# A down product of a mixture-of-experts arm, cut into three parts that stand in three places

## The chip, the cores and the metric

The kernel runs on one core of a Trainium2 chip. The metric is the device time of one execution in microseconds (us). Before the change the median of 3 runs is 892.29 us (890.97 to 893.22).

## The reference

Three layers follow each other. What matters here is the second: each of 1792 tokens goes to the one expert of eight that its gate picks, if its skip score is positive.

```python
x = attn_out.transpose(0, 2, 1, 3).reshape(1792, 768)   # sigmoid attention, 12 heads
do_compute = (x @ w_skip) > 0
xc = x[do_compute]
probs = softmax(xc @ w_gate)                            # 8 experts
e_idx, gate_w = argmax(probs), max(probs)
for e in range(8):
    mask = e_idx == e
    h = np.maximum(xc[mask] @ w1[e], 0.0)               # 768 -> 1024
    y[mask] = gate_w[mask, None] * (h @ w2[e])          # 1024 -> 768
x[do_compute] = xc + y
# then a dense layer over all rows: g = elu(x @ w_in), out = g @ w_out   (768 -> 2048 -> 768)
```

With the inputs that are timed, the chosen tokens per expert are 0, 65, 199, 144, 391, 35, 10 and 222.

## The kernel before, in words

Every matrix product is made of three fp32r products (high by high, high by low, low by high), so that `gemm` (L593 to L596) issues three matmuls: L594, L595, L596.

The expert stage works on blocks of up to 256 tokens of one expert: two halves of 128 rows. A first block is taken early; the others are ordered by how many rows they hold, and a branch per block picks one of three arms. `k = 3` (the "many" arm) has more than 64 rows in the second half, `k = 2` (the middle arm, "few") has 1 to 64, `k = 1` has none. By the counts above, the blocks after the first are two "many" arms, two middle arms and three arms with one half. **Only the two middle arms execute changed code**; they are blocks 3 and 4.

The weights of an expert come in eight chunks of 128 x 1536: chunks 0 to 3 are the up weights, 4 to 7 the down weights. A chunk is loaded by SyncE (L550), and split into a high part on ScalarE (L585) and a low part on VectorE (L587). A down chunk holds 4 slices of 128 hidden rows and 384 output columns. Chunk 4, the fifth, holds hidden slices 0 to 3 and output columns 0 to 383.

A middle arm runs in this order on TensorE:

1. `up_parts`: the up products, first the full half (3 matmuls per slice, into `acc0` and `acc1`), then the few rows. The few rows' high and low parts stand side by side in one operand, so two matmuls per slice do for them (L959, L960).
2. `back` of chunks 4 and 5 for the few rows.
3. `h_columns(1)`: the turns of h. The second 512 hidden columns of the full half are transposed (L142, 4 matmuls) and those of the few rows turned and folded (L930, 4 matmuls of two passes each), into PSUM tiles `pt0` and `pt1`. ScalarE takes the relu and rounds it (L937), VectorE makes the low part (L938), both into the tile `both`.
4. `back` of chunks 6 and 7 for the few rows. These need what L938 wrote. After each of the two, ScalarE copies the sum to SBUF (L1027, `yf`).
5. `back` of chunk 4 for the full half: four slices of three matmuls, into `acc2`. Its inputs are hidden slices 0 to 3, turned much earlier, and the split chunk 4.
6. `outcome`: the fold. Two fp32 matmuls (L1094, two passes each) add the two parts of the few rows, from `yf` into `acc0` and `acc1`, and VectorE multiplies by the gate and adds to the rows (L1095, twice).

The other chunks of the full half (5, 6, 7) are done in the next block, beside its first steps.

Behind the arm comes the control flow. The arm that is not taken is replaced by `rest()`, a tiny matmul (L1257), ScalarE copy (L1258) and VectorE copy (L1259), which keep the semaphore counts of all paths alike. On each engine the sequencer jumps over the code of the untaken arms: L1275 is the branch of the "few" arm, L1279 that of the "many" arm, L1266 asks whether the next block has rows. The next block begins with transposes of its gathered rows (L142, out of `xg`) into `pt0`, `pt1` and `acc1`.

The order of the instructions on TensorE, ScalarE and VectorE is the order in which they are written (`manual_schedule`).

Of the kernel before, what the change touches and what calls it, by code (L numbers as in the profile page):

```python
# [23 lines left out]
P = 128  # L24
# [10 lines left out]
KF1 = F1 // P  # L35
# [6 lines left out]
N2 = DM // 2  # L42
WCH = 1536
# [48 lines left out]
def build(nc, tc, a):  # L92
# [3 lines left out]
    with ExitStack() as top:  # L96
# [44 lines left out]
        def flip(dst, src):  # L141
            nc.tensor.transpose(dst, src, ident)  # L142
# [34 lines left out]
        with ExitStack() as st:  # L177
# [411 lines left out]
            def weights(i, c):  # L589
                j = (8 * i + c) % NSPL  # L590
                return whi_t[j], wlo_t[j]

            def gemm(o, a_hi, a_lo, b_hi, b_lo, first, last):  # L593
                nc.tensor.matmul(o, a_hi, b_hi, start=first, stop=False)  # L594
                nc.tensor.matmul(o, a_hi, b_lo, start=False, stop=False)  # L595
                nc.tensor.matmul(o, a_lo, b_hi, start=False, stop=last)  # L596
# [159 lines left out]
            py = [[acc_t[j][:, :N2] for j in js] for js in ((2, 3), (4, 1))]  # L756
# [165 lines left out]
            def h_columns(nh, sizes):  # L922
                for h, n in enumerate(sizes):
                    pt = pt_t[(nh + h) % 2].rearrange("p (c n) -> p c n", c=4)[:, :, :n]
                    for j in range(4):
                        w = slice(j * P, (j + 1) * P)
                        if n == P:
                            flip(pt[:, j, :], hs_t[nh][:, w])
                        else:
                            nc.tensor.matmul(  # L930
                                pt[:, j, :], hf_t[nh][:, w], fold[:, :n], start=True, stop=True
                            )
                    t = slice(h * P, h * P + n)
                    h_hi, h_lo = h2[:, nh, 0, :, t], h2[:, nh, 1, :, t]
                    if n < P:
                        h_lo = h2[:, nh, 0, :, h * P + n : (h + 1) * P]
                    nc.scalar.activation(h_hi, pt, AF.Relu)  # L937
                    nc.vector.scalar_tensor_tensor(  # L938
                        h_lo, pt, 0.0, h_hi, op0=ALU.max, op1=ALU.subtract
                    )  # L940
# [4 lines left out]
            def h_part(s, k):  # L945
                return h2[:, k // 4, s, k % 4]

            def product(o, h, n, a2, i, c, width, k0, total):

                t = slice(h * P, (h + 1) * P)  # L950
                for j in range(WCH // width):
                    w = slice(j * width, (j + 1) * width)
                    hi, lo = (u[:, w] for u in weights(i, c))
                    a_hi, a_lo = (a2(s, k0 + j)[:, t] for s in range(2))
                    first, last = k0 + j == 0, k0 + j == total - 1
                    if n == P:
                        gemm(o, a_hi, a_lo, hi, lo, first, last)
                    else:
                        nc.tensor.matmul(o, a_hi, hi, start=first, stop=False, skip_group_check=True)  # L959
                        nc.tensor.matmul(  # L960
                            o[:n], a_hi[:, :n], lo, start=False, stop=last, skip_group_check=True
                        )
# [55 lines left out]
                        else:  # L1018
                            nc.scalar.copy(hf_t[nh], acc_t[(3, 0)[nh]])

            def back(i, h, n, chunks):

                for c in chunks:
                    c4, nh = divmod(c - 4, 2)
                    product(py[nh][h], h, n, h_part, i, c, N2, 4 * c4, KF1)
                    if n < P and c4:
                        nc.scalar.copy(yf_t[nh], py[nh][h])  # L1027

# [25 lines left out]
            def expert(i, k, sizes, following=None):  # L1054
                whole = sizes == (P, P)

                def soon():
                    outcome(i - 1, 0, P)

                if whole:  # L1060
                    up_two(i, soon)
                    ahead(i, 4)
                else:
                    up_parts(i, sizes, soon)
                    if len(sizes) > 1:
                        skips(f"many{i}", 1 - (k >> 1))
                    elif i + 1 < NB:
                        skips(f"more{i + 1}", (following + 3) >> 2)
                ahead(i, 5)
                for h, n in list(enumerate(sizes))[1:]:  # L1070
                    if whole:
                        back(i, h, n, range(4, 8))
                        outcome(i, h, n)
                        back(i, 0, P, range(4, 5))
                    else:
                        back(i, h, n, range(4, 6))
                        h_columns(1, sizes)
                        back(i, h, n, range(6, 8))
                        back(i, 0, P, range(4, 5))
                        outcome(i, h, n)  # L1080
                if len(sizes) == 1:
                    back(i, 0, P, range(4, 5))
                    h_columns(1, sizes)

            def outcome(i, h, n):
                gated(xg_t[i % NXG][h], slot_gate[:, 2 * i + h : 2 * i + h + 1], h, n)
# [441 lines left out]
```

## Time and profile before

| | us |
|---|---|
| median of 3 runs | 892.29 |
| the profiled execution | 889.8 |
| span of the profiled execution | 888.0 |
| busy TensorE in the span | 867.5 |
| first middle arm, up products to the last transposes of the next block | about 271 to 301 |
| second middle arm | about 307 to 336 |

The profile is one execution. A timeline row gives the start, the length, the engine, the line of the kernel, the operation with its output and inputs, and how often; in square brackets stands how long the engine was idle before it, and which instruction's end released it. The length of a matmul is modelled and overlaps the next one: the distance between starts tells the pace. Rows with "q" behind an engine's name are instructions of that engine's sequencer (PEldq is TensorE's), which are not counted as busy.

### The profile page before, as it was taken

To read this page: it belongs to the slowest core of one execution; us is meant where nothing else is said; L and a number is where in the kernel's file an instruction comes from. 1 tells how busy PE (TensorE), PEld (TensorE's weight loads), DVE (VectorE), ACT (ScalarE), POOL (GpSimd) and SP (SyncE) were. 2 spreads that over 40 slices of the span, in tenths; PEclk is the share of its full clock that TensorE was granted. 3 is DMA by queue.
4 is the path that set the end of the run, shared out by engine and by line. 5 is a ranking of instruction groups with operands and counts; after the bars stand their busy time and mean duration, and the time that the engine had idled before them with its cause. 6 is when DMAs were issued, how large, how long until landed. Compare 5 with 4: busy or idle time off the path is not lost.

```text
span 888.0 us, 13671 instructions
## 1 busy us (share of the span) xinstructions
PE 867.5 (98%) x5206; PEld 705.1 (79%) x5206; DVE 555.1 (63%) x872; ACT 476.3 (54%) x680; POOL 82.8 (9%) x79
## 2 busy tenths in 40 slices
PE   9999999999999899999999999999999999999998
PEld 6544454899998787888888888888888888888997
DVE  4878777886656648885888875443434434334664
ACT  7876776545346447764545454443443434434664
POOL 1000001021120213351000000000000100000100
PEclk9999999999999999999999999999999999999999
DMA  9898976789772538927733330100010100000100
GB/s 331 268 317 308 314 275 198 285 334 405 273 258 90 190 155 342 410 92 245 237 88 108 107 108 19 54 1 18 19 35 19 54 1 1 1 1 18 54 1 37
DMA packets 37842, 134.71 MB, mean 152 GB/s; under 512 B 5082, under 2 KB 9306, under 8 KB 37746
## 3 DMA queue, kind: packets, MB, share of 16 engines
q1 hardware_dynamic: 33122, 114.26, 36.0%
q0 software_dynamic: 4480, 19.01, 6.0%
q8 instruction: 56, 0.92, 0.4%
q14 instruction: 40, 0.33, 0.1%
q10 hardware_dynamic: 144, 0.20, 0.1%
HBM read 112.47 MB, written 23.99 MB: 154 GB/s over the span
## 4 chain that ended last, share of the span: by engine, by line
PE 54%; DVE 0%; ACT 0%; issue 0%; ACTq 0%
PE acc L1393 16%; PE pt L1393 10%; PE acc L1361 9%; PE acc L1362 9%; PE acc L1360 9%; PE acc L142 1%; PE acc L1244 0%; PE acc L594 0%; PE acc L596 0%; PE acc L595 0%; DVE both L611 0%; ACT both L609 0%; ACT raw L1404 0%; ACTq L1524 0%; ACTq L609 0%
## 5 line engine op out<-in xcount | busy, mean ns | idle before, releaser
L587 DVE TENSOR_TENSOR wlo<-raw,whi 128x1536 fp32r<-128x1536 f32 x64 | 111.4, 1758 | 29.4 <-ACT whi L585 28.8
L1371 DVE SCALAR_TENSOR_TENSOR m<-m,acc 128x512 f32<-128x512 f32 (+1 forms) x64 | 39.7, 620 | 139.4 <-ACT m L1370 139.4
L1369 ACT ACTIVATE m<-acc 128x512 f32<-128x512 f32 (+1 forms) x64 | 34.9, 545 | 168.6 <-PE acc L1362 158.6
L250 ACT ACTIVATE at<-ps,bias 128x896 f32<-128x896 f32 x96 | 82.7, 918 | 37.6 <-PE ps L297 34.7
L585 ACT CAST whi<-raw 128x1536 fp32r<-128x1536 f32 x64 | 94.0, 1482 | 16.2 <-PE acc L596 5.4
L1393 PE MATMUL acc<-wol,gh 128*128 128x256 f32 x320 | 100.8, 315 | 0.0
L1393 PE MATMUL acc<-woh,gl 128*128 128x256 f32 x320 | 100.4, 314 | 0.0
L1393 PE MATMUL acc<-woh,gh 128*128 128x256 f32 x320 | 100.4, 314 | 0.0
L1361 PE MATMUL acc<-x,wih 128*128 128x512 f32 (+1 forms) x270 | 96.2, 356 | 0.0
L1360 PE MATMUL acc<-x,wih 128*128 128x512 f32 (+1 forms) x270 | 96.2, 356 | 0.0
L1362 PE MATMUL acc<-x,wil 128*128 128x512 f32 (+1 forms) x270 | 96.1, 356 | 0.0
L594 PE MATMUL acc<-whi,both 128*128 128x384 f32 (+1 forms) x236 | 83.9, 355 | 1.8 <-DVE both L611 1.8
L595 PE MATMUL acc<-wlo,both 128*128 128x384 f32 (+1 forms) x236 | 82.9, 351 | 0.6 <-DVE wlo L587 0.6
L596 PE MATMUL acc<-whi,both 128*128 128x384 f32 (+1 forms) x236 | 82.6, 350 | 0.0
L1349 DVE TENSOR_TENSOR wol<-wo,woh 128x768 fp32r<-128x768 f32 x64 | 61.2, 956 | 23.4 <-ACT woh L1348 23.0
L1393 PEld LDWEIGHTS acc<-woh,gh 128*128 128x128 f32 x320 | 60.3, 188 | 10.0
L1393 PEld LDWEIGHTS acc<-wol,gh 128*128 128x128 f32 x320 | 60.3, 188 | 9.4
L1348 ACT CAST woh<-wo 128x768 fp32r<-128x768 f32 x64 | 53.4, 834 | 25.9 <-PE acc L1393 25.9
L1375 DVE TENSOR_TENSOR gl<-m,gh 128x512 fp32r<-128x512 f32 (+1 forms) x64 | 40.0, 626 | 40.5 <-ACT gh L1374 40.5
L1393 PEld LDWEIGHTS acc<-woh,gl 128*128 128x128 f32 x320 | 60.1, 188 | 4.2
L1343 DVE TENSOR_TENSOR wil<-wi,wih 128x768 fp32r<-128x768 f32 x60 | 57.4, 956 | 7.6 <-ACT wih L1342 6.9
L1374 ACT CAST gh<-m 128x512 fp32r<-128x512 f32 (+1 forms) x64 | 36.3, 567 | 46.0 <-DVE m L1371 46.0
(272 smaller groups left out, 1910.4 us busy)
## 6 DMA issues: line engine op xcount, KB each, us to landing
raw<-in_w SPq DMA_DIRECT2D x66, 768.0 KB, 12.0
raw<-in_wi SPq DMA_DIRECT2D x9, 768.0 KB, 5.6
raw<-in_wo SPq DMA_DIRECT2D x9, 768.0 KB, 6.7
raw<-in_wi SPq DMA_DIRECT2D x14, 384.0 KB
raw<-in_wo SPq DMA_DIRECT2D x14, 384.0 KB, 3.1
qr<-in_q SPq DMA_DIRECT2D x11, 448.0 KB, 6.9
vt<-in_v SPq DMA_DIRECT2D x12, 384.0 KB, 5.9
x_d<-xr SPq DMA_DIRECT2D x12, 384.0 KB, 6.5
```

The lines of the kernel that those rows point to most:

```text
L250: nc.scalar.activation(out, ps, AF.Sigmoid, bias=bias, scale=QK_SCALE)
L585: nc.scalar.copy(w_hi, raw)
L587: nc.vector.tensor_sub(w_lo, raw, w_hi)
L594: nc.tensor.matmul(o, a_hi, b_hi, start=first, stop=False)
L595: nc.tensor.matmul(o, a_hi, b_lo, start=False, stop=False)
L596: nc.tensor.matmul(o, a_lo, b_hi, start=False, stop=last)
L1343: nc.vector.tensor_sub(pair[1], raw, pair[0])
L1349: nc.vector.tensor_sub(pair[1], wo_r[f], pair[0])
L1360: nc.tensor.matmul(o, a, b, start=(cc == 0), stop=False)
L1361: nc.tensor.matmul(o, a, c, start=False, stop=False)
L1362: nc.tensor.matmul(o, wil[:, cc], b, start=False, stop=(cc == KD - 1))
L1393: nc.tensor.matmul(o, a, b, start=(clears and f == 0 and k_ == 0), stop=(f == KF2 - 1 and k_ == 2), skip_group_check=True,)
```

## The change

`product` and `back` take a slice of the four steps of a chunk. In the middle arm the full half's chunk 4 (twelve matmuls into `acc2`) is cut in three: two steps behind the turns of h and in front of the few rows' chunks 6 and 7, one step behind these, and one step behind the fold.

```diff
-            def product(o, h, n, a2, i, c, width, k0, total):
+            def product(o, h, n, a2, i, c, width, k0, total, part=slice(None)):
...
-                for j in range(WCH // width):
+                for j in range(WCH // width)[part]:
...
-            def back(i, h, n, chunks):
+            def back(i, h, n, chunks, part=slice(None)):
...
-                    product(py[nh][h], h, n, h_part, i, c, N2, 4 * c4, KF1)
+                    product(py[nh][h], h, n, h_part, i, c, N2, 4 * c4, KF1, part)
...
                         back(i, h, n, range(4, 6))
                         h_columns(1, sizes)
+                        back(i, 0, P, range(4, 5), slice(0, 2))
                         back(i, h, n, range(6, 8))
-                        back(i, 0, P, range(4, 5))
+                        back(i, 0, P, range(4, 5), slice(2, 3))
                         outcome(i, h, n)
+                        back(i, 0, P, range(4, 5), slice(3, 4))
```

Only TensorE's order changes; it has as many instructions as before, and those of the other engines stand as they stood. The lines of the changed kernel below the arm carry numbers that are higher by 2.

The first place is on TensorE behind the turns of h, in a middle arm. `acc2` is the full half's sum, `acc3` one of the few rows', `whi0`/`wlo0` the split chunk 4 and `whi2`/`wlo2` chunk 6.

```order
 L142 MATMUL pt1_1883<-cst_79,hs1_2297 128x128 x4
 L930 MATMUL pt0_1882<-cst_79,hf1_2299 128x64 x4
+L594 MATMUL acc2_1886<-whi0_1812,both_117 128x384
+L595 MATMUL acc2_1886<-wlo0_1813,both_117 128x384
+L596 MATMUL acc2_1886<-whi0_1812,both_117 128x384
+L594 MATMUL acc2_1886<-whi0_1812,both_117 128x384
+L595 MATMUL acc2_1886<-wlo0_1813,both_117 128x384
+L596 MATMUL acc2_1886<-whi0_1812,both_117 128x384
 L959 MATMUL acc3_1887<-whi2_1893,both_117 128x384
 L960 MATMUL acc3_1887<-wlo2_1894,both_117 64x384
```

Six matmuls now stand between the turns and the first matmul that needs what L938 makes of them.

The second place is on TensorE at the arm's end, where `acc0` and `acc1` take the fold, and the branch leaves the arm.

```order
-L594 MATMUL acc2_1886<-whi0_1812,both_117 128x384
-L595 MATMUL acc2_1886<-wlo0_1813,both_117 128x384
-L596 MATMUL acc2_1886<-whi0_1812,both_117 128x384
-L1094 MATMUL acc0_1884<-hf0_2298,cst_79 128x384
-L1094 MATMUL acc1_1885<-hf1_2299,cst_79 128x384
-L1275 UNCONDITIONAL_BRANCH
...
+L1096 MATMUL acc0_1884<-hf0_2298,cst_79 128x384
+L1096 MATMUL acc1_1885<-hf1_2299,cst_79 128x384
+L594 MATMUL acc2_1886<-whi0_1812,both_117 128x384
+L595 MATMUL acc2_1886<-wlo0_1813,both_117 128x384
+L596 MATMUL acc2_1886<-whi0_1812,both_117 128x384
+L1277 UNCONDITIONAL_BRANCH
```

The fold stood behind all twelve matmuls of chunk 4; now nine of the twelve stand before it, six of those before the few rows' last chunks, and three stand between the fold and the branch.

## Rows read from the trace of the kernel before

**Rows 1.** The page's head and its first part: busy us (share), instructions.

```profile
span 888.0 us, 13671 instructions
PE 867.5 (98%) x5206; PEld 705.1 (79%) x5206; DVE 555.1 (63%) x872; ACT 476.3 (54%) x680; POOL 82.8 (9%) x79
```

**Rows 2.** The instructions of L960: count, ns min/median/max, first and last start.

```profile
L960 PE MATMUL acc<-wlo,both x56: 332/337/394, 273.3 to 329.9; 128*64 128x384 f32 x32, 128*64 128x512 f32 x24
```

**Rows 3.** The timeline of TensorE, first middle arm, turns of h to next block.

```profile
289.29 1.00 PE L930 MATMUL pt<-cst,hf 128*128 128x64 f32 x8
291.23 0.44 PE L959 MATMUL acc<-whi,both 128*128 128x384 f32 x1 [0.94 <-DVE both L938]
...
294.12 0.34 PE L594 MATMUL acc<-whi,both 128*128 128x384 f32 x1
...
296.20 1.45 PE L1094 MATMUL acc<-hf,cst 128*128 128x384 f32 x4
297.49 0.17 PE L1257 MATMUL acc<-iota_h 128*128 128x2 f16 x1
299.37 1.06 PE L142 MATMUL pt<-cst,xg 128*128 128x128 f32 x8 [1.72 <-DVE rest L1259]
```

**Rows 4.** The same of the second middle arm.

```profile
325.24 1.00 PE L930 MATMUL pt<-cst,hf 128*128 128x64 f32 x8
327.18 0.44 PE L959 MATMUL acc<-whi,both 128*128 128x384 f32 x1 [0.93 <-DVE both L938]
...
330.05 0.34 PE L594 MATMUL acc<-whi,both 128*128 128x384 f32 x1
...
332.14 1.45 PE L1094 MATMUL acc<-hf,cst 128*128 128x384 f32 x4
333.43 0.17 PE L1257 MATMUL acc<-iota_h 128*128 128x2 f16 x1
334.57 1.09 PE L142 MATMUL pt<-cst,xg 128*128 128x128 f32 x8 [0.98 <-DVE rest L1259]
```

**Rows 5.** The timelines of VectorE and ScalarE, first middle arm.

```profile
290.12 1.05 DVE L938 SCALAR_TENSOR_TENSOR both<-pt,both 128x512 fp32r<-128x512 f32 x2
...
298.22 0.14 DVE L1259 COPY rest<-cst 128x1 f32<-128x1 f32 x1
...
294.37 0.48 ACT L1027 COPY hf<-acc 128x384 f32<-128x384 f32 x1 [0.61 <-PE acc L960]
```

**Rows 6.** The same of the second middle arm.

```profile
326.07 1.05 DVE L938 SCALAR_TENSOR_TENSOR both<-pt,both 128x512 fp32r<-128x512 f32 x2
...
334.37 0.15 DVE L1259 COPY rest<-cst 128x1 f32<-128x1 f32 x1
...
330.31 0.48 ACT L1027 COPY hf<-acc 128x384 f32<-128x384 f32 x1 [0.91 <-PE acc L960]
```

**Rows 7.** The timeline of TensorE behind the earlier turns of h.

```profile
281.74 1.00 PE L930 MATMUL pt<-cst,hf 128*128 128x64 f32 x8
282.56 0.48 PE L594 MATMUL acc<-whi,both 128*128 128x512 f32 x1
```

**Rows 8.** Branches of TensorE's sequencer (L1275, L1279) at the first middle arm's end.

```profile
L1275 PEldq COMPARE_BRANCH  x1: 218/218/218, 294.9 to 294.9; - x1
L1279 PEldq COMPARE_BRANCH  x2: 444/1816/3189, 295.2 to 295.7; - x2
```

**Rows 9.** Branches of L1279 at the second middle arm's end.

```profile
L1279 PEldq COMPARE_BRANCH  x2: 200/275/350, 331.1 to 331.5; - x2
```

**Rows 10.** Branches of L1279 from 225 to 262 us, the "many" arms.

```profile
L1279 PEldq COMPARE_BRANCH  x3: 63/197/201, 225.9 to 260.4; - x3
```

**Rows 11.** DMA queues from 295.7 to 298.9 us: packets, MB, share.

```profile
q8 instruction: 1, 0.02, 2.2%
```

**Rows 12.** What TensorE waited for from 335 to 412 us: total, times, longest.

```profile
PE pt L142 <- DVE both L938: 4.7, 3, 1.7
PE acc L594 <- DVE both L611: 1.8, 1, 1.8
```

## The prediction

> **What bounds the kernel now.** I read the busy table first: TensorE is busy 867.5 of 888.0 us, so it is the bound almost everywhere, and only its 20.5 us of idle time can be won by a change of order [rows 1]. Next, who runs the changed code: an instruction that only middle arms have, L960, ran 56 times, 24 on 512 and 32 on 384 columns, and one arm issues 12 and 16 [rows 2]. So there are two middle arms, and every gain or loss of mine is counted twice at most. Then TensorE's timeline through both arms [rows 3, 4]. Each shows two idle gaps. The first, behind the turns of h, is 0.94 and 0.93 us and ends when VectorE's L938 ends (290.12 + 1.05 = 291.17, and L959 starts at 291.23; in the second arm 327.12 and 327.18) [rows 3 to 6]. The second, at the start of the next block, is 1.72 and 0.98 us, and the profile puts both down to the VectorE copy L1259 [rows 3, 4].
>
> That releaser has to be checked against the copy's own end. In the second arm L1259 ends at 334.52 and the transposes start at 334.57: it is the releaser [rows 4, 6]. In the first arm it ends at 298.36, but the transposes start at 299.37, 1.0 us later [rows 3, 5]. What ended last there stands among the sequencer's branches: two branches of L1279, at 295.2 and 295.7 us, of 444 and 3189 ns. A sequencer takes one at a time, so the second is the long one: 295.7 to 298.9 [rows 8]. The same branches took 350 and 200 ns behind the second arm and at most 201 ns in the "many" arms [rows 9, 10]. In the long one's time the instruction queue moved one packet of 0.02 MB [rows 11]: the sequencer most likely waited for code. **So the two arms end on different things: the first on TensorE's own branch, the second on the chain fold, gate, L1259.**
>
> **Part by part.**
>
> *Six matmuls behind the turns.* The turns leave TensorE's pace 0.82 us after the start of L930's eight passes (281.74 to 282.56 with a matmul right behind) [rows 7]. So the first moved matmul can start at 289.29 + 0.82 = 290.11. One of this shape takes 0.173 us: twelve from 294.12 to 296.20 [rows 3]. It reads hidden slices turned long before, waits for nothing new, and after the gap may cost 0.1 more (0.44 against 0.34 for the first behind a gap) [rows 3]. Six last 1.04 to 1.14 and end at 291.15 to 291.25, against 291.23 where L959 is released anyway. They fit the gap; L938 itself does not move, as ScalarE and VectorE do nothing new. Cost: 0 to 0.07 us, since L959's weights can be loaded only once it is released. In the gap these six come free.
>
> *The wait that stays.* L959 still waits for L938, and behind it on TensorE stand the few rows' 16 matmuls. They start as before and last as before, 291.23 to 294.12, or 0.1 less if the engine is no longer coming out of a gap [rows 3].
>
> *Up to the fold.* Before, twelve matmuls stood between them and the fold; now three. The fold starts 9 x 0.173 = 1.56 us earlier, or 1.66 with the 0.1; I take 1.6. It needs both `yf` copies. The second ends at 294.85, or 0.1 earlier [rows 5]; the fold's first half then runs from about 294.6 for half of 1.29 us, so the second half, at 295.2, finds its copy done. No new wait, with 0.3 us to spare.
>
> *Behind the fold.* Three matmuls, 0.52 us, and L1257. Its start moves from 297.49 by 1.6 - 0.52 = 1.08 us to an earlier time. VectorE's two gate products and L1259 follow the fold and move by the whole 1.6 us; the three matmuls write another tile than they read, `acc2`.
>
> *Second arm.* The next block's transposes start at the later of three: L1259's end plus 0.05, so 334.57 - 1.6 = 332.97; TensorE's last matmul, 333.43 + 0.17 - 1.08 = 332.52; the sequencer. Its second branch of L1279 began at 331.5 and took at most 0.35 [rows 9]; in the first arm 0.47 us passed from the long branch's end (298.9) to the transposes [rows 3, 8], which makes it ready at about 332.3. The first branch, L1275, began at 294.9 in the first arm, 0.05 after the second `yf` copy ended [rows 5, 8]: the sequencer had stood at the fold and had everything in front of it issued. Now three matmuls come between the fold and that branch; none of my rows shows an issue alone, so I bound it by 0 and by their execution, 0.52. Ready then at 332.2 to 332.8: below 332.97 in either case. **Gain 1.6 us.**
>
> *First arm.* Here the long branch is the end. It moves with the second `yf` copy (0 to 0.1 earlier) and the three issues (0 to 0.52 later): between 0.1 earlier and 0.5 later. If it takes its 3.19 us again, the transposes start at 299.3 to 299.9 instead of 299.37. I take 0.2 later, near the middle. L1257 done 1.08 and L1259 done 1.6 us earlier then buy nothing. **Loss 0.2 us.**
>
> [...]
>
> *Behind the arms.* From 335 to 412 us TensorE waited for two things alone, L938 and L611 at the blocks' ends, 6.5 us in all [rows 12]: chains that start from TensorE itself and move with it. No wait there ends on a transfer, so a block that begins 1.4 us earlier passes it on to the dense stage. SyncE's loads and GpSimd's scatter behind L1259 start earlier too, by 1.6 us; nothing waits less or more for them.
>
> *Sum.* 1.6 - 0.2 = 1.4 us off the profiled execution, 889.8 to 888.4. The median stands 2.49 us above that execution; with the same shift, 892.29 to **890.9**.
>
> **The rivals.**
>
> A. *The long branch is gone in the new order.* For it: of seven branches of L1279 in [rows 8 to 10] one is long, and its timing against the fetches changes a little. Against it: the code is as long and the sequencer comes to it within half a microsecond of before. The first arm would then end like the second, on L1259: 298.36 - 1.6 + 0.05 = 296.8 instead of 299.37, a gain of 2.56. With the second arm 4.2 us: 888.1.
>
> B. *The long branch belongs to the profiled execution and not to the timed ones.* For it: one execution is all that the profile shows. Against it: that execution is faster than all three timed ones. Then both arms end on L1259 before and after, and the gain is 2 x 1.6 = 3.2: 889.1.
>
> C. *Slower: the second arm gets a long branch.* Its branch of 331.5 comes 0 to 0.5 later and takes 3.19; 0.47 behind it the transposes start, at 335.2 to 335.7 instead of 334.57. This decides from a branch of about 0.9 us on (332.97 - 0.47 - 331.6), and from 2.5 us on the arm loses. Price 0.9, and 0.2 in the first arm: 893.4. For it: the first arm shows that such a stall exists at this branch. Against it: the distance between the branches and the code is unchanged.
>
> D. *Given back later.* The next block starts earlier and waits for its weights instead: 892.3. The waits behind the arms speak against it: none ends on a load [rows 12].
>
> **How the numbers follow.** My forecast 0.60, A 0.13, B 0.12, C 0.08, D 0.07. [...] The forecast's own range is 889.7 to 892.1: 0.3 us either way for the terms above, and about 1 us for a median of a few runs that spread over 2.25 us. The range from 888.3 to 892.8 takes in B, D and the forecast and cuts A and C in part. A measurement of this kernel tells about 0.3% from no change, 2.7 us. Faster by more than that: all of A, two thirds of B, a little of the rest, 0.23. Slower by more: C falls short of it, so that only a second such stall would do, 0.05. Within: 0.72.
>
> **What would show it.** TensorE without a gap between L930 and L959 in both arms; the fold 1.6 us earlier against L938; the second arm's transposes 1.6 us earlier against L938 and released by L1259; the branch of L1279 behind the first arm still about 3.2 us long, with the transposes 0.5 us after its end although L1259 ended more than 2 us before. Wrong: if that branch is short (then A), if one appears behind the second arm (C), if L959 starts more than 0.1 us later against L938, or if the fold waits for L1027.

## The result, and the profile after

The changed kernel takes 901.07 us (median of 17 runs, 892.93 to 904.17) against 891.12 for the kernel before (17 runs, 887.67 to 893.22): a ratio of 1.0097, 95% interval 1.008 to 1.0114. The prediction was 890.9 with a range up to 892.8, so it was wrong: some nine microseconds slower by the ratio, not 1.4 faster. The profiled execution took 902.31 us, its span is 900.5 against 888.0. In the changed kernel the lines below the arm stand two lower: L1096 is the fold (before L1094), L1097 the gate products, L1259 and L1261 the rest of TensorE and VectorE, L1281 the "many" test, L1274 the "two" test (before L1272), L1277 the "few" test.

The page's first part, after (against [rows 1]) and its row of TensorE's granted clock in 40 slices:

```profile
span 900.5 us, 13671 instructions
PE 871.5 (97%) x5206; PEld 708.6 (79%) x5206; DVE 555.7 (62%) x872; ACT 476.2 (53%) x680; POOL 73.4 (8%) x79
...
PEclk9999999999999799999999999999999999999999
```

TensorE is 4.0 us longer busy with the same instructions and idle 29.0 instead of 20.5 us. Its timeline through the first arm, then through the second and the block behind it (against [rows 3, 4]):

```profile
288.88 1.00 PE L930 MATMUL pt<-cst,hf 128*128 128x64 f32 x8
289.69 0.42 PE L594 MATMUL acc<-whi,both 128*128 128x384 f32 x1
...
290.82 0.44 PE L959 MATMUL acc<-whi,both 128*128 128x384 f32 x1
...
294.22 1.45 PE L1096 MATMUL acc<-hf,cst 128*128 128x384 f32 x4
...
298.22 0.18 PE L1259 MATMUL acc<-iota_h 128*128 128x2 f16 x1 [2.02 <-issue]
305.23 1.94 PE L142 MATMUL pt<-cst,xg 128*128 128x128 f32 x8 [6.83 <-issue]
```

```profile
339.10 1.45 PE L1096 MATMUL acc<-hf,cst 128*128 128x384 f32 x4
...
341.54 1.09 PE L142 MATMUL pt<-cst,xg 128*128 128x128 f32 x8 [0.44 <-DVE rest L1261]
...
351.33 0.44 PE L594 MATMUL acc<-whi,both 128*128 128x384 f32 x1 [3.73 <-issue]
```

VectorE, first and second arm (against [rows 5, 6]): L938, whose end opens L959, and the copy L1261.

```profile
289.71 1.05 DVE L938 SCALAR_TENSOR_TENSOR both<-pt,both 128x512 fp32r<-128x512 f32 x2
...
296.24 0.14 DVE L1261 COPY rest<-cst 128x1 f32<-128x1 f32 x1
...
334.59 1.05 DVE L938 SCALAR_TENSOR_TENSOR both<-pt,both 128x512 fp32r<-128x512 f32 x2
...
341.33 0.15 DVE L1261 COPY rest<-cst 128x1 f32<-128x1 f32 x1
```

What the six matmuls were to do is there: no gap between L930 and L959, and the fold 3.46 us behind L938's end in both arms (290.76 to 294.22, 335.64 to 339.10), where it was 5.03 and 5.02. The second arm's transposes come 5.9 us behind L938's end instead of 7.45. The loss is at three places where TensorE waits for "issue", its own sequencer: 2.02, 6.83 and 3.73 us. The sequencer's branches (count, ns min/median/max, first and last start), L1281 behind the first and the second arm and L1274 in the block behind the second (against [rows 8, 9]), and below them L1272 of the kernel before, the same test as L1274:

```profile
L1281 PEldq COMPARE_BRANCH  x2: 3271/4850/6429, 294.9 to 298.2; - x2
...
L1281 PEldq COMPARE_BRANCH  x2: 200/275/350, 339.7 to 340.2; - x2
...
L1274 PEldq COMPARE_BRANCH  x1: 5859/5859/5859, 345.4 to 345.4; - x1
```

```profile
L1272 PEldq COMPARE_BRANCH  x1: 1770/1770/1770, 338.4 to 338.4; - x1
```

Before, one long branch (3189 ns [rows 8]) and one of 1770 that TensorE did not wait for at all (no wait for issue stands in [rows 12]); after, 3271, 6429 and 5859. Waits of TensorE from 335 to 412 us (against [rows 12]):

```profile
PE pt L142 <- DVE both L938: 4.5, 3, 1.5
PE acc L594 <- issue: 3.7, 1, 3.7
PE pt L142 <- DVE rest L1261: 0.4, 1, 0.4
```

Then the clock. Two windows (busy us of the five engines, granted clock, DMA share, GB/s), the first from within the wait of 6.83 us on, the second right behind the one of 3.73:

```profile
300.70:310.80 10.10, 5.57 (x22) 5.60 (x23) 2.83 (x4) 3.13 (x4) 2.97 (x3) 0.50 1.01 415
351.90:355.20 3.30, 3.30 (x12) 3.30 (x11) 0.05 (x1) 0.01 (x1) 1.04 (x2) 0.50 1.02 413
```

The granted clock stood at 0.50 there, from 300.65 for 10.24 us and from 351.85 for 3.41; eight transposes took 1.94 us instead of 1.06. Before, all of this stretch ran at 1.00. The ledger of the profiled executions, each place as after minus before:

- L938's end in the first arm 290.76 for 291.18: -0.4
- from there to the next block's transposes 14.47 for 8.20: +6.3
- on to L938's end in the second arm 30.41 for 27.75 (half clock): +2.7
- on to the transposes 5.89 for 7.45: -1.6
- the block behind, to the start of the next one, 26.87 for 21.13 (branch and half clock): +5.7
- the rest: -0.2. Sum 12.5, the difference of the spans.

The last thing to see stands at SyncE and at the queues. Its first weight load for the next block is issued 0.12 us behind VectorE's rest, before and after:

```profile
298.48 2.74 SPq L550 DMA_DIRECT2D raw<-in_w  x3
```

```profile
296.50 2.74 SPq L550 DMA_DIRECT2D raw<-in_w  x3
```

Before, the long branch had its one packet of code at 296.30, ahead of those loads. After, the branch of 298.24 comes behind them: the loads are 2.0 us earlier, and the branch is 2.5 us later than before (295.70), since the one of 3271 ns stands ahead of it. The queues of the kernel after from 298.2 to 304.7 us, the time of that branch (packets, MB, share; against [rows 11]):

```profile
q1 hardware_dynamic: 338, 1.89, 76.3%
q0 software_dynamic: 80, 0.39, 14.5%
q8 instruction: 1, 0.02, 0.9%
```

The code packet starts at 302.28, 4.0 us behind its branch, between 338 packets of weights; in the first branch, with the queues empty, it came 0.7 us behind (294.89 and 295.60).

### The profile page after: what moved, and what is told of

The parts are those of the page before. It is cut to its first block, busy times and chain, and to the rows that moved or that the text cites. A ratio compares the mean times of both kernels' runs of the same rounds, so it can differ in the third digit from the quotient of the medians.

```text
span 900.5 us, 13671 instructions
## 1 busy us (share of the span) xinstructions
PE 871.5 (97%) x5206; PEld 708.6 (79%) x5206; DVE 555.7 (62%) x872; ACT 476.2 (53%) x680; POOL 73.4 (8%) x79
## 4 chain that ended last, share of the span: by engine, by line
PE 54%; ACT 0%; ACTq 0%; issue 0%
PE acc L1395 16%; PE pt L1395 10%; PE acc L1363 9%; PE acc L1364 9%; PE acc L1362 9%; PE acc L142 1%; PE acc L1246 0%; PE acc L594 0%; PE acc L596 0%; PE acc L595 0%; ACT raw L1406 0%; ACTq L1526 0%
## 5 line engine op out<-in xcount | busy, mean ns | idle before, releaser
L594 PE MATMUL acc<-whi,both 128*128 128x384 f32 (+1 forms) x236 | 86.0, 365 | 5.6 <-issue 3.7
L596 PE MATMUL acc<-whi,both 128*128 128x384 f32 (+1 forms) x236 | 83.8, 355 | 0.0
L271 PE MATMUL po<-at,vt 128*64 128x448 f32 (+1 forms) x324 | 59.5, 505 | 1.5 <-DVE xT L302 1.5
```

Of the source, the lines that this page charges most:

```text
L271: nc.tensor.matmul(po[half(j), o : o + step], vt[0][:, 2 * (n % 2) + j, c, :], at[:, 2 * c + j, o : o + step], start=(c == o == 0), stop=F ...
```

## The experiments

Every kernel ran beside the kernel before on the same chip. The table gives, of one profiled execution of each, the time from L938's end to the next block's transposes (first arm, second arm), the length of the block behind the second arm, the branches (the two of the "many" test at the first arm's exit; the test L1272/L1274 behind the second arm), all in us, and the ratio of the times with its 95% interval.

| kernel | 1st tail | 2nd tail | block behind | exit branches | test behind | ratio to before |
|---|---|---|---|---|---|---|
| before | 8.20 | 7.45 | 21.13 | 0.44, 3.19 | 1.77 | 1 |
| after | 14.47 | 5.89 | 26.87 | 3.27, 6.43 | 5.86 | 1.0097 (1.0080-1.0114) |
| e1 six in front only | 13.41 | 6.42 | 27.99 | 3.23, 5.42 | 5.89 | 1.0112 (1.0076-1.0148) |
| e2 three behind only | 8.49 | 6.94 | 22.41 | 0.45, 3.47 | 3.08 | 1.0003 (0.9989-1.0016) |
| e3 after, shifted | 8.24 | 5.90 | 26.80 | 0.45, 3.21 | 5.79 | 1.0119 (1.0086-1.0153) |
| e4 before, shifted | 8.11 | 7.45 | 22.38 | 0.44, 3.05 | 2.94 | 1.0008 (0.9997-1.0019) |
| e5 twelve loads out | 13.96 | 5.90 | 28.10 | 3.01, 6.21 | 6.41 | 1.0080 (1.0048-1.0112) |
| e6 loads later | 7.96 | 5.90 | 27.60 | 0.45, 2.93 | 3.37 | 1.0074 (1.0049-1.0098) |
| e7 before, code moved | 7.25 | 7.46 | 20.91 | 0.35, 0.20 | 0.45 | 0.9993 (0.9979-1.0006) |
| e8 after, code moved | 5.68 | 5.89 | 28.25 | 0.35, 0.20 | 6.37 | 1.0031 (1.0017-1.0044) |
| e9 after, no loads | 11.91 | 5.90 | 22.21 | 3.03, 4.13 | 3.71 | 1.0026 (1.0006-1.0045) |
| e10 before, no loads | 7.94 | 7.46 | 20.92 | 0.45, 2.93 | 1.02 | 0.9984 (0.9971-0.9997) |
| e11 e8, loads 2.4 later | 5.68 | 5.90 | 26.81 | 0.34, 0.20 | 5.59 | 1.0062 (1.0043-1.0082) |
| e12 after again | 8.42 | 5.89 | 28.45 | 0.45, 3.39 | 6.35 | 1.0091 (1.0064-1.0119) |
| s1 first arm only | 13.86 | 7.45 | 21.17 | 3.38, 5.73 | 1.81 | 1.0066 (1.0040-1.0093) |
| s2 second arm only | 8.07 | 5.90 | 28.02 | 0.44, 3.05 | 5.92 | 1.0042 (1.0025-1.0059) |
| s3 no hint | 14.20 | 5.89 | 26.95 | 3.33, 6.10 | 5.84 | 1.0114 (1.0086-1.0143) |
| s4 hint in the arm | 8.32 | 5.90 | 26.86 | 0.45, 3.29 | 5.93 | 1.0105 (1.0072-1.0137) |
| s5 s2 and a wait | 8.03 | 8.71 | 22.63 | 0.44, 2.97 | 2.63 | 1.0050 (1.0032-1.0067) |
| s6 after and two waits | 8.50 | 8.71 | 22.67 | 0.45, 3.03 | 2.70 | 1.0078 (1.0056-1.0100) |

One thing holds in all of these profiles. Each branch of TensorE's sequencer over 0.9 us between 285 and 350 us, 42 in all, ends 2.3 to 2.8 us behind the start of a packet of code on q8. So these branches wait for code, and how long each takes says when its packet started: from 1.3 us ahead of the branch (e10, 1.02 us) to 4.1 behind it (e5, 6.41 us).

**Which part, and is it the place of the code?** e1 keeps the six matmuls in front and lets the other six stand ahead of the fold; e2 keeps the three behind it alone. e3 and e4 shift TensorE's code behind their line by three warm-up matmuls.

```diff
e1 -  back(i, 0, P, range(4, 5), slice(2, 3))
   +  back(i, 0, P, range(4, 5), slice(2, 4))
      outcome(i, h, n)
   -  back(i, 0, P, range(4, 5), slice(3, 4))
e2 -  back(i, 0, P, range(4, 5), slice(0, 2))
      back(i, h, n, range(6, 8))
   -  back(i, 0, P, range(4, 5), slice(2, 3))
   +  back(i, 0, P, range(4, 5), slice(0, 3))
e3 -  keep_warm(25)
   +  keep_warm(28)          (in the kernel after)
e4 -  keep_warm(25)
   +  keep_warm(22)          (in the kernel before)
```

> Chunk 4 of the full half in two parts only: two steps behind the turns of h, the other two in front of the fold; nothing stands between the fold and the branch. Theory 1 (the loss comes from the three matmuls behind the fold: TensorE's sequencer waits at the fold's second half for the last copy of L1027, and it now stands six instructions further from the branch there, so that the code behind the branch is asked for only when the branch itself comes): the branches behind the first arm are as in the kernel before (one of about 3.2 us), no idle gap over 2 us, each fold 1.04 us earlier against L938; the second arm gains 1.0, the first nothing: about 1.0 us faster than the kernel before. Theory 2 (the loss comes from the six matmuls in front of L959, which let the sequencer wait at another place there): both long branches, gap of 6 to 7 us behind the first arm, 8 to 12 us slower than the kernel before.

> Chunk 4 of the full half with three steps in front of the fold and one behind it; nothing stands in the wait for L938. Theory 1 (the three matmuls behind the fold): two long branches of 3 and 6 us behind the first arm, 6 to 7 us of idle TensorE there and half the clock for some us after it, 8 to 12 us slower than the kernel before. Theory 2 (the six in front of L959): branches as in the kernel before; the second arm's end moves 0.52 us earlier, the first arm's not: 0.3 to 0.7 us faster.

> The changed kernel with three more of the warming matmuls at its start (28 for 25), which do nothing for the result; each has a weight load, so all the code of TensorE behind them stands six instructions later, and the wait at the fold stands at the place in the code where it stands in the kernel before. The three cost at most 0.6 us at the start. Theory 1 in its form a (place in the code): the branches are as in the kernel before, each fold 1.6 us earlier, 1 us faster than the kernel before. Theory 1 in its form b (distance from the wait to the branch): the distance is as in the changed kernel, two long branches, 8 to 12 us slower. Theory 2: as the changed kernel, 8 to 12 us slower, if it goes by order; it cannot tell if by place.

> The kernel before with three warming matmuls fewer at its start (22 for 25): all the code of TensorE behind them stands six instructions earlier, and the wait at the fold stands at the place in the code where the changed kernel has it, with the order untouched. Theory 1 form a (place in the code): the first branch behind the first arm misses as in the changed kernel, 6 to 7 us idle, 8 to 12 us slower than the kernel before, without any move of a product. Theory 1 form b (distance to the branch) and theory 2: within 0.6 us of the kernel before.

e1 loses as much as the whole change and has its branches; e2 takes the time of the kernel before. The three behind the fold cost nothing that the times show, the six in front carry the loss. e2's test behind the second arm takes 3.08 us and costs TensorE a wait of 1.2, but so does e4's (2.94 and 1.2), which has the order of before. The shifts do not undo the loss and do not make it, though in e3's profiled execution the first exit branch is short, where two long ones were expected. L1280 is the "many" test in e1:

```profile
L1280 PEldq COMPARE_BRANCH  x2: 3227/4326/5424, 293.9 to 297.2; - x2
```

**What do the branches wait for?** e5 leaves twelve weight loads out, e6 makes five of each block's six wait for the last matmul of the step ahead of the test; e7 and e8 write 87 matmuls that are never run into an arm that no row takes, which moves the code behind it. In these and the next code cuts, "..." stands for lines left out.

```diff
e5 -  fetch(i, range(2, 8))
   +  if i not in (4, 5):
   +      fetch(i, range(2, 8))
e6    ...                     (last_mm[0] is gemm's last matmul)
   -  fetch(i, range(2, 8))
   +  late = 3 if i in (4, 5) else 8
   +  fetch(i, range(2, late))
      between(i)
   +  if late < 8:
   +      fetch(i, range(late, 8), after=[last_mm[0]])
e7, e8 (of before, of after; block 1, the one-half arm)
   +  for _ in range(87):
   +      nc.tensor.matmul(acc_t[5][:, :2], iota_h, iota_h[:, :2], start=True, stop=True)
```

> The changed kernel, with the twelve weight loads that SyncE issues at the start of the blocks behind the two middle arms left out (chunks 2 to 7 of these two blocks are not loaded, so the result of those blocks is not the reference's). Theory 3, contention: the six matmuls bring the loads ahead of TensorE's request for the code behind its jump, and the 16 KB packet stands behind them. Then without the loads the jump at the end of the first middle arm takes about 3.2 us, not 6.4, and the one in the block behind the second arm 1.8 to 3.1, not 5.9; TensorE's clock is not at half behind either; the profiled execution comes out some 8 us below the changed kernel's 902.3, at 892 to 895. The first of the two long jumps (3.27) may stay. Theory 4, order alone: what the six matmuls change is the state of TensorE's code buffer, and the loads have no part in it; then the jumps stay at 6.4 and 5.9 and the time at 899 to 903.

> The changed kernel, with five of the six weight loads of the two blocks behind the middle arms made to wait for the last matmul of the step ahead of the block's first jump, some 6 us later; all the work is done. Theory 3, contention: the code packets come before the loads, the jump at the end of the first arm takes about 3.2 us and the one in the block behind the second arm 1.8 to 3.1; the profiled execution comes out 6 to 9 us below the changed kernel's 902.3, less up to 2 us for each block that waits for its fourth chunk: 893 to 898. Theory 4, order alone: jumps of 6.4 and 5.9, time 899 to 905.

> The kernel before, with 87 matmuls that are never run (an arm of block 1 that no row takes) written into TensorE's code, so that its code from block 2 on lies 174 instructions further on. Theory 5, place: the 3.2 us of the jump at the end of the first arm hang on where jump and target lie in the code; with this shift that jump takes 0.5 us or less and the kernel is about 2.5 us faster, at 886.5 to 888. Its rival: it is a matter of what was fetched when, or another jump becomes long in its place; then the time is the same as before to 0.3%, or longer.

> The changed kernel with the same 174 instructions that are never run. Theory 3 with theory 5: the jump at the end of the first arm needs no fetch, so nothing stands behind the loads there; about 9 us come off at that place, and the block behind the second arm either keeps its 5.7 us (time about 893) or loses them too (887). Theory 4: long jumps stay, 899 to 903, whatever the place.

e5 kept its 6.21 and 6.41, which seemed to fell the contention. But it had not taken the transfers away: SyncE issued the following blocks' loads in their place, from 296.85 us on, and 273 packets of weights lay beside the second branch's one of code. It decided nothing. In e6 the test behind the second arm takes 3.37, as contention has it. The 2.93 of its first arm tell less: the first exit branch was short there, and behind a short one the second took 3.21 to 3.39 with the loads unmoved too (e3, s4, e12). The loads that came too late then cost TensorE another 3.3 us, which the table's 27.60 holds. e7 and e8 show that the place counts as well: with the code moved, the first arm has no long branch at all (0.35 and 0.20 us), before or after, and e8's first tail of 5.68 is 2.5 us under that of before. e7's first tail is only 0.95 us under before, for without the long branch it ends on L1259. Nor is e7 faster than before: other branches became long elsewhere (3.54 us at 233.2; 2.52 at 378.7, behind which TensorE waited 1.15 for issue). And in e8 the one behind the second arm stays at 6.37, enough for 1.0031.

e9 and e10 take the transfers away in earnest: no load at all from block 4's third chunk on. e11 is e8 with the loads behind the last cast of the next block's columns, e12 is the changed kernel once more.

```diff
e9, e10 -  if i == NB:
        +  if i == NB or i > 4 or (i == 4 and chunks[0] == 2):
               return
e11     ...                              (the 87 matmuls of e8; last_cast)
        -  fetch(i, range(2, 8))         (of blocks 4 and 5; block start)
        +  fetch(i, range(2, 8), after=[last_cast[0]])   (behind columns(i, ends))
```

> The changed kernel without any weight load from block 4's third chunk on (the blocks behind the first middle arm compute with what lies in the buffers, so the result is not the reference's). In the run without twelve loads the next blocks' loads were issued at the same place, so the transfers were still there; here none is. Theory 3, contention with the loads: the second jump at the end of the first middle arm takes about 3.1 us instead of 6.4, and the one in the block behind the second arm 3.4 or less instead of 5.9, since the code packet comes at most 1 us after the branch. Theory 4, order alone: the packet still comes 3 to 4 us after the branch and the jumps stay at 6.4 and 5.9.

> The kernel before without the same weight loads (the result is not the reference's). It tells when TensorE's code for the jump in the block behind the second middle arm is asked for. If it is asked about 3.3 us after the packet that follows the hint, ahead of the branch (theory 3a), the packet comes at that time, 3.3 us behind the first, and the jump takes 0.5 us or less, in this kernel and in the changed one alike. If it is asked at the branch (theory 3b), the packet comes 0.6 to 1.0 us after the branch and the jump takes about 3 us in both.

> The changed kernel with the 174 instructions that are never run, and with the six loads of each of the two blocks behind the middle arms made to wait for the last cast behind the block's transposes, about 2.4 us later; all the work is done. Theory 3a: the code packet for the jump in the block behind the second arm is then ahead of the loads, the jump takes under 1 us (6.37 in the run without the wait), no clock is lost, and the two arms' 3.1 us stay gained: 885 to 887, below both kernels. Theory 3b: the packet comes 1 us after the branch or later, the jump takes 3.3 to 6 us, and the time is 889 to 893.

> The changed kernel itself again, for a second profiled execution and more times. If the long jumps are a matter of timing within an execution, they are not the same in each: the first jump at the end of the first middle arm takes 3.3 us in some executions (time about 902) and 0.4 in others (about 894 to 897). If they hang on code and place alone, this one shows 3.27, 6.43 and 5.86 us again.

The sequencer's branches of e9, at the first arm's exit and behind the second arm, and what TensorE waited for from 335 to 350 us:

```profile
L1281 PEldq COMPARE_BRANCH  x2: 3027/3578/4129, 295.0 to 298.1; - x2
...
L1274 PEldq COMPARE_BRANCH  x1: 3712/3712/3712, 341.2 to 341.2; - x1
```

```profile
PE acc L594 <- issue: 0.9, 1, 0.9
PE pt L142 <- DVE rest L1261: 0.4, 1, 0.4
```

Without loads the second exit branch takes 4.13 instead of 6.43, the one behind the second arm 3.71 instead of 5.86; its packet starts 1.0 us behind the branch, not 3.5, TensorE loses 0.9 us there instead of 3.7, and the block takes 22.21 instead of 26.87. The weight loads make up 2.2 to 2.3 us of each of the two branches. Both stay above the 3.1 and 3.4 expected: the second exit branch's packet comes 1.8 us behind it, and in between lie 80 packets of GpSimd's gather, which e9 leaves in. The first exit branch keeps its 3.03 without any load about. In e10 the packet for the test behind the second arm comes ahead of its branch:

```profile
L1272 PEldq COMPARE_BRANCH  x1: 1024/1024/1024, 337.5 to 337.5; - x1
```

The packet starts at 336.21, the branch at 337.51. So the kernel before asks for that code earlier than at the branch; in e9 the 1.0 us behind the branch is no more than the 0.6 to 1.1 that a packet took on empty queues elsewhere, so that the changed kernel seems to ask about at the branch. My 3a, a request 3.3 us behind the last packet whatever the kernel does, is wrong (4.0 in e10, 4.7 in e9), and e11 fell with it: loads only 2.4 us later were issued from 336.06 on, just ahead of the branch at 336.66, and the branch took 5.59; the time, 896.31, lies above both forecasts.

e12 differs from the profiled execution of the same kernel: its first exit branch is short.

```profile
L1281 PEldq COMPARE_BRANCH  x2: 453/1924/3394, 294.5 to 295.0; - x2
...
L1274 PEldq COMPARE_BRANCH  x1: 6349/6349/6349, 336.4 to 336.4; - x1
```

The second branch then starts at 295.00, ahead of the loads, has its packet at 295.58 and takes 3.39. A code packet at 291.57, which the other execution lacks, goes with the short branch. That holds in all profiles whose code is not moved by the 87 matmuls: with a packet of the queue q8 between 290 and 294 us the first exit branch takes 0.44 or 0.45, without it 3.0 to 3.4. With the six matmuls in the first arm it is long in 6 of 11 profiles (after, e1, e5, e9, s1, s3, not e3, e6, e12, s4, s6), without them in none of 6 (before, e2, e4, e10, s2, s5). The times go with it: of the kernels that cut both arms and do no more than shift code or change the hint, the profiled executions with the long branch took 901.5 to 903.0 us (after, e1, s3), those with the short one 893.4 to 896.7 (e3, e12, s4). That goes far to explain the 11 us over which the times of the changed kernel spread. The branch behind the second arm is long in all six.

**Which arm, the hint, and the interval.** s1 and s2 cut the chunk in one arm alone. s3 leaves out the prefetch hint of block 5's "two" test (BRANCH_PREFETCH_HINT in the trace, an instruction of 28 to 42 ns ahead of a branch), s4 moves it into the second arm. s5 (on s2) and s6 (on the changed kernel) make VectorE's last copy behind the arm later by 18 copies of one column.

```diff
s1, s2 +  cut = (0, 2, 3, 4) if i == 3 else (0, 0, 4, 4)     (s2: i == 4)
       ...                                   (the three slices from cut)
s3     +  if i != 5:
              skips(f"two{i}", k >> 1)
s4        back(i, 0, P, range(4, 5), slice(0, 2))
       +  if i == 4:
       +      skips(f"two{i + 1}", following >> 1)
       ...                                   (and none at block 5's start)
s5, s6 -  nc.vector.tensor_copy(next(rest_t[1]), cst[:, :1])
       +  last = next(rest_t[1])
       +  for _ in range(1 + more):              (more = 18 behind the cut arms)
       +      nc.vector.tensor_copy(last, cst[:, :1])
```

> The chunk is cut in the first middle arm alone; the second has the order of before. If the arms' losses are their own: the first arm's transposes come 8.4 us behind its turns (jump of 3.4) or 14 us behind (3.3 and 6.4, clock at half), the second arm's and the jump behind it are as before (packet ahead of the branch or up to 1 us behind, 1.8 to 3.1 us): 889 to 890 in the good executions, 897 to 899 in the others. If the jump behind the second arm is upset by anything earlier, it takes 5.9 us here too: 895 and above in all.

> The chunk is cut in the second middle arm alone. If the arms' losses are their own: the first arm and its jump are as before, the second arm is 1.6 us shorter, and the jump in the block behind it takes 5.4 to 6.4 us with its packet 3 to 4 us behind the branch, TensorE's clock at half behind it: 5.5 to 7 us lost there, 892 to 895. If the loss needs the first arm's upset: 887 to 888.

> The changed kernel without the prefetch hint for the jump in the block behind the second middle arm. Theory 6, hint: the hint starts the fetch of the jump's code and now stands 4.8 us ahead of the branch instead of 6.3; without it the packet comes at the branch or behind it as now, and the jump takes as long or longer (5.9 to 6.5). Theory 7: the hint's fetch gets in the way of the running order's; without it the jump becomes shorter, 0.5 to 3.5.

> The changed kernel with the hint for the jump in the block behind the second middle arm given some 5 us earlier, inside the second arm, behind the first six matmuls. Theory 6, hint: its fetch goes before the loads, the jump takes under 0.5 us, no clock is lost behind it, and some 6 us come back: 889 in an execution without the first arm's 6.4 us jump, 895 to 897 in one with it. Theory 7, or if a hint given so early is lost at the jumps in between: the jump stays at 5.8 to 6.5, or the arm's own exit jump takes 3.2 us in its place.

> The chunk cut in the second middle arm alone, and 18 more copies of one column on VectorE behind that arm, which make its last copy 1.2 to 2.6 us later (the gain of the arm is given away; loads and transposes start as late as before or later). Theory 8, interval: with the wait back between the sequencer's entry into the block and the loads, the code packet of the jump behind the arm comes ahead of the branch or within 1 us of it, the jump takes 1.8 to 3.1 us or less and the clock stays whole: 889 to 891, though VectorE does more. Theory 9, order: the matmuls' new order makes the packet late; the jump stays at 5.4 to 6.4, and the time is 894 to 897.

> The changed kernel with the 18 copies behind both middle arms. Theory 8: both jumps are as in the kernel before, except where the first arm's first jump is long of itself (3.3 us, in more than half of the executions of the changed kernel); behind that one the second jump takes about 3.2 us and not 5.4 to 6.4, as the loads come later than its request: 889 to 892, and 892 to 895 with the long first jump. Theory 9: 900 to 904 as in the changed kernel, or more.

Each arm's loss is its own: s1 has the first arm's long branches and 1.81 us behind the second, as before; s2 the reverse. Neither arm alone is worth having (1.0066 and 1.0042). The hint has no part in it: without it 5.84, given 12 us ahead 5.93. Over all profiles the test behind the second arm takes 0.45 to 3.08 us where the six matmuls are not in that arm, and 5.6 to 6.4 where they are, except in the two that took all loads away or put most of them behind the test (e9, e6) and the two with a wait (s5, s6). The branch behind the second arm in s2, and in s5, where TensorE's instructions stand in the same order and VectorE's last copy is later; s5's copies and TensorE's waits from 325 to 350 us:

```profile
L1275 PEldq COMPARE_BRANCH  x1: 5917/5917/5917, 335.2 to 335.2; - x1
```

```profile
L1277 PEldq COMPARE_BRANCH  x1: 2634/2634/2634, 340.8 to 340.8; - x1
```

```profile
333.37 3.54 DVE L1264 COPY rest<-cst 128x1 f32<-128x1 f32 x19
```

```profile
PE pt L142 <- DVE rest L1264: 3.3, 1, 3.3
```

The copies took 3.54 us, more than the 1.2 to 2.6 expected. But the packet comes 0.3 us behind the branch instead of 3.5, the branch takes 2.63, and TensorE waits for no code at all. The block goes from 28.02 to 22.63 us, although the 3.3 us idle ahead of it are followed by 3.41 us at a granted clock of 0.50.

What s5 changed is seen by counting from the hint, which the sequencer passes as it enters the block (332.03 in before, 340.65 in the changed kernel, 332.61 in s5) to the packet of the test's code (337.52, 348.91, 341.14). The first weight loads of the block, in before, after and s5:

```profile
334.64 5.13 SPq L550 DMA_DIRECT2D raw<-in_w  x4
```

```profile
341.60 2.32 SPq L550 DMA_DIRECT2D raw<-in_w  x3
```

```profile
335.33 8.14 SPq L550 DMA_DIRECT2D raw<-in_w  x7
```

| us behind the hint | before | after | s5 |
|---|---|---|---|
| first load issued | 2.6 | 1.0 | 2.7 |
| test reached | 6.3 | 4.8 | 8.2 |
| packet of its code starts | 5.5 | 8.3 | 8.5 |

The loads are back at the distance of before, but the packet is as late as in the changed kernel. It is the test that comes later, and so waits less. So s5 shows that a late packet costs little when the test comes late as well, with the matmuls in the changed order. It does not show that the shorter interval makes the packet late, nor does it clear the matmuls' order of that. s6 has the same behind the second arm, 2.70; its first arm is no test, since its first exit branch was short, and its 3.03 is near what came behind a short one without a wait.

The medians, 894.06 for s5 and 896.12 for s6, lie above what theory 8 said (889 to 891, and 889 to 892 with a short first branch). In s5's profile the second tail is 1.3 us and the block 1.5 us longer than before. Both waits cost more than the cut had gained, and none of the runs that did all the work beats the kernel before by more than can be measured.

## Why the prediction was wrong

*Six matmuls behind the turns*, *the wait that stays*, *up to the fold*, *behind the fold*: right. No gap, the fold 1.57 us earlier against L938 where 1.6 was said, and no wait for L1027. *Second arm*: right as far as it went, 7.45 to 5.89, a gain of 1.56 for 1.6, and released by the copy L1261.

Two terms failed. *First arm*: "between 0.1 earlier and 0.5 later", loss 0.2. In e12 that is what happened, 8.42 for 8.20. In the profiled execution the sequencer waited for code twice (3.27 and 6.43 us), the tail grew by 6.3, and the half clock behind it cost 2.7 more; by the profiles above this comes in about half of the executions. The prediction held the 3.19 us to be a fixed price that would either be paid again or not, an estimate from one branch of one execution. It is a transfer's wait: 0.6 to 1.1 us to the packet on empty queues, 4.0 us once a first long branch (3.27) had put the second behind weights that the change itself had brought forward.

*Behind the arms* is the term that failed in both profiled executions of the changed kernel: "SyncE's loads and GpSimd's scatter behind L1259 start earlier too, by 1.6 us; nothing waits less or more for them." TensorE's sequencer does, for its code. I had read [rows 12] as a list of all that could wait there. That list names what ended an idle time of the kernel before. A branch of 1.77 us was hidden there behind matmuls already issued, so it stood in no row of waits, and I did not list the sequencer's branches beyond the arms. Made 5.86, it cost TensorE 3.73 us and then 3.41 us of half clock: 5.7 together (7.3 in e12), against a gain of 1.6. Some 2.2 us of the branch are the weight loads (e9); the rest comes of the code being asked for later than before.

Of the rivals, C came nearest: slower by a long branch behind the second arm. It stood one test too early (L1279, which stayed at 350 and 200 ns), and its price of 0.9 and 0.2 took no account of queued transfers or of the clock. The sum also had no term for the clock at all; 2.7 us behind the first arm are its work alone. A's price was right where its condition was made: in e8, without the long branch, the first tail is 2.52 us under before, where A said 2.56.

In the trace the code comes over another queue than the weights (q8 against q1); in the changed kernel its packet started 0.7 us behind its branch on empty queues and 3.5 to 4.0 us behind it beside the weights. The place of the code counts, for with the code moved both exit branches of the first arm were short (0.35 and 0.20 us, e7 and e8), but it is not all: one and the same kernel had its first exit branch at 3.27 us in one execution and at 0.45 in another (after, e12).

What stays open: why the code for the test behind an arm is asked for ahead of the branch in the kernel before and at or behind it in a cut arm (the matmuls' order and the shorter interval go together in every run but s5 and s6, and those do not tell them apart), and why, with the six matmuls in the first arm, its first exit branch is short in some executions of a kernel and 3.3 us in others, with no transfers about.

## What to carry to other kernels

Before work is moved into a gap, ask which DMA issues hang on what then becomes earlier, and what else asks the DMA engines for something in the next few microseconds; code for TensorE's jumps is one of these (here one packet of 16 KB, which beside the weight loads started 3.5 to 4.0 us behind its branch and not 0.7). List every branch of the critical engine's sequencer with its duration, the hidden ones too: a branch like the 1.77 us here, which cost nothing, is cover almost used up (2.94 cost 1.2). And where a profile shows a wait of several microseconds for issue, look for the granted clock behind it before the price is written down (0.50 for 10.24 and for 3.41 us here).

## What the runs showed of the hardware

- At the first arm's exit a branch with a packet of code behind its start took 2.9 to 3.5 us on empty queues (3.19 in before, 3.27 in after, 2.93 in e10); the packet, of 16 KB, came 0.6 to 1.1 us behind it and took 0.9 to 1.4. Where weight loads put the packet 3.1 to 4.1 us behind the branch, here or at the test behind the second arm, the branch took 5.4 to 6.4 (6.43 and 5.86 in after, 5.42 in e1, 6.41 in e5). In both cases it ended 2.3 to 2.8 us behind the packet's start.
- Some 1.8 to 2.8 us of the branch behind the second arm are covered by matmuls already issued: 1.77 us cost TensorE nothing (before), 2.94 cost 1.2 (e4), 3.71 cost 0.9 (e9), 5.86 cost 3.7 (after).
- An idle time of 3.3 us behind a busy stretch (s5, for VectorE) and of 3.7 us (after, for code) were each followed by 3.41 us at a granted clock of 0.50; with 2.0 and 6.8 us in short order (after) it lasted 10.24. An idle time of 2.8 us in e3 was followed by 3.41 us of it as well, one of 3.0 us in e12 by none.
- A prefetch hint at 5 us or 12 us ahead of the jump, or none, made no difference to it (5.86, 5.93, 5.84 us).
- 19 copies of one column took 3.54 us on VectorE in a row, 0.19 us each, where one alone shows 0.14 to 0.15.
